# Nine second-layer products of each slot behind the join of its forms, and a new order of gathers and weight loads on GpSimd

## The chip, the cores and the metric

The kernel runs on one core of a Trainium2 chip. The metric is the device time in microseconds of one execution; the kernel before took 573.17 us (median of 3 runs, 572.85 to 578.56).

## The reference

Two stages, in fp32. First a block-local attention: q, k and v of 8 batches, 8 heads, 576 rows and head size 64; each chunk of 64 rows attends to itself alone, so a score block is 64x64. The result is laid out as x, 4608 rows of 512. Then a mixture of 8 experts, of which each row takes the one with the largest logit:

```python
logits = x @ w_gate
expert_idx = np.argmax(logits, axis=1)
gate_w = probs[np.arange(N), expert_idx]
for e in range(E):
    mask = expert_idx == e
    h = np.maximum(x[mask] @ w1[e], 0.0)      # 512 -> 1024
    out[mask] = gate_w[mask, None] * (h @ w2[e])   # 1024 -> 512
```

How many rows each expert gets is known only while the kernel runs.

## The kernel before, in words

The first 150 us do the attention, the routing and a scatter of the rows of x into a DRAM table sorted by expert (`xd`). What follows is a loop over **slots**, unrolled in the program: slot u takes 256 rows of one expert through both layers, and the last slot of an expert takes up to 192 leftover rows with them. Every operand is split into a high and a low fp32r part, so that a product of matrices is three products: hi x hi, hi x lo, lo x hi.

The code of a slot has four **forms**, of which a branch at its start picks one by the number of leftover rows (`kind`): `form_x` for 128 leftover rows (called EXT below), for 192 (EXW), for 64 (HALF), and `form_a` without any. They stand in the program in this order, and after them comes the **common part**, where the four join. In a form, first-layer columns f = 0 to 7 are computed one after another (`gemm1`, L674, or `gemm1_x`, L681; 12 matmuls each), ScalarE makes `hh` (relu, L701) and VectorE `hl` (L706) of each, and the second-layer products of column f - 2 (`block`: for each of two row halves m, three matmuls of 512 columns, L767 to L769, into psU or psV) stand between. Columns 4 and 5 (`block(4)`, `block(5)`, six matmuls each) end the form. The common part holds columns 6 and 7 of the first half (six matmuls); those of the second half (`rest`) stand in the next slot, behind its branch, for slots below 12 (`SMIN`), and in the common part from 12 on. An EXT or EXW form ends with a jump (L1317) over the forms behind it to the common part, HALF with one at L1316, `form_a` falls through. The branch at a slot's start is L1315.

In the run that is profiled, `form_a` is taken by slots 2, 3, 4, 6, 8, 11, 13, 14 and 15, HALF by 1, 5 and 7, EXW by 9 and 12, EXT by 10.

Each engine runs its own instructions in the order of the program (a manual schedule). The rows of slot u + 2 are gathered on GpSimd (`gather(u + 2)`, two indirect DMAs into `xg4[:, 2:4]`, L600), and the leftover rows of slot u + 1 too (`gather_x(u + 1)`, into `xg3` and `xg5`, L600). `load_w(u, c)` (L573) is one indirect DMA for 1 MB of weights into `raw[c]`; ScalarE and VectorE split them (L82, L83) in `split_step` and in the common part. `spread(u + 1)` at a slot's start is 16 DMAs of the SP queue (L643) that rearrange `xg4[:, 2:4]` into `xg4[:, 0:2]`; `turn` (L649, VectorE, at f = 5) transposes the latter, and `make_xs` (L654, L655) in the common part splits it into `xhl`, the input of the next slot. So `gather(u + 2)` can only start once `spread(u + 1)` has been read out. For slot 2, the common part of slot 1 uses transposes on TensorE (`make_xt(2)`, L625) in place of `turn` and `make_xs`. The leftover rows go through TensorE transposes at the start of a form (L663).

GpSimd also issues the outputs (`finish`, L799) and has a `drain` at the start of the common part. DMA completions of GpSimd are counted on eight semaphores in turn; a reader waits for the count of the one that its DMA got.

Of the kernel before, what the change touches and what calls it, by code (L numbers as in the profile page):

```python
# [40 lines left out]
XW = D + 16  # L41
HB = 3
WARM = 36
PLACE = {1: 87, 2: 110, 3: 110}
BLOCK = 256
SKEW = 128
BIG = 1.0e6
# [3 lines left out]
def attn_moe_kernel(ctx: ExitStack, tc: tile.TileContext, q, k, v, wg, w, w0, out):  # L51
# [27 lines left out]
    def split_chunk(par, c):  # L79
        hi, lo = w_hi[par][c], w_lo[par][c]  # L80
        src = raw[c // 2][:, (c % 2) * 1024:(c % 2 + 1) * 1024]
        nc.scalar.copy(hi, src)  # L82
        nc.vector.tensor_tensor(lo, src, hi.bitcast(F32), ALU.subtract)  # L83
# [20 lines left out]
    def bank(tag, shape):  # L104
        n = 1
        for x in shape[1:]:
            n *= x
        if tag == "S":
            t = psum[0].tile([P, 512], F32, name="psS", tag="S", bufs=2)
        else:  # L110
            t = slots[tag][turns[tag] % len(slots[tag])]
            turns[tag] += 1
        t = t[0:shape[0], 0:n]
        if len(shape) == 3:
            t = t.rearrange("p (a b) -> p a b", b=shape[2])
        return t
# [451 lines left out]
    def wset(u):  # L568

        return 0 if u < 2 else (u + 1) % 2  # L570

    def load_w(u, c):
        nc.gpsimd.indirect_dma_start(  # L573
            out=raw[c][:, :], out_offset=None,
            in_=w, in_offset=bass.IndirectOffsetOnAxis(ap=widx[:, u, c:c + 1], axis=0),
            bounds_check=4 * E * P - 1, oob_is_err=False)
# [10 lines left out]
    def rows_of(u):  # L587
        return xg[0] if u in (0, 2) else xg[1]
# [9 lines left out]
    def rows_in(t, u, h):  # L598
        rows = TE[u] * P if u < 2 and h < 2 else NT
        nc.gpsimd.indirect_dma_start(  # L600
            out=t[:, :], out_offset=None, in_=xd[0:rows, :],
            in_offset=bass.IndirectOffsetOnAxis(ap=place(u, h)[0:t.shape[0], :], axis=0),
            bounds_check=rows - 1, oob_is_err=False)

    def gather(u):
        for h in range(2):
            rows_in(rows_of(u)[h], u, h)

    def gather_x(u):
        rows_in(xg3, u, 2)  # L610
        rows_in(xg5, u, 3)
# [25 lines left out]
    def spread(u):  # L637

        for h in range(2):
            ids(u, rows_of(u)[h], h)  # L640
        for a in range(4):
            for b in range(4):
                nc.sync.dma_start(  # L643
                    xq.rearrange("p (h a) x -> p h a x", a=4)[b * 32:(b + 1) * 32, :, a, :],
                    xg4[a * 32:(a + 1) * 32, 2:4, b * P:(b + 1) * P])
# [77 lines left out]
    def slot_0():  # L723

        py = None
        for i, step in enumerate(BLOCKS):
            f = BLOCKS[:i].count(step)
            flush()
            if step == "1":
                ph = bank("S", [P, BLK])  # L730
                gemm1_pe(0, f, ph, range(2))
                yield
                gemm1_pe(0, f, ph, range(2, 4))
                lo_.append((ph, relu_hi(ph)))
            else:
                if py is None:
                    py = [bank(x, [P, D]) for x in "UV"]
                gemm2(0, f, h0[f], 0, py)
                if f == 7:
                    finish(0, 0, py[0])  # L740
                    last.append(py)
                    return
                yield
                gemm2(0, f, h0[f], 1, py)
            yield
# [13 lines left out]
    fill, halves = slot_0(), [2 * len(BLOCKS)]  # L759

    def gemm2(par, f, h, m, py):
        gemm2_pe(par, f, *(x[:, m * P:(m + 1) * P] for x in h), py[m])
# [41 lines left out]
    def split_step(u, i):  # L804

        if i < 2:
            if u < 2:
                load_w(u + 1, 2 + i)
                return
            split_chunk(wset(u), 6 + i)  # L810
            if i == 1:
                load_w(u + 1, 3)
                load_w(u + 1, 2)
        else:
            split_chunk(wset(u + 1), i - 2)
            if i % 2:
                load_w(u + 2, i // 2 - 1)
# [40 lines left out]
    def find_u(u):  # L858
        return find(idx[u % 3], rowm[:, u, :], rowm[:, u, :], KB - 1) if u < NU else iter(())
# [353 lines left out]
    h_of = h0[5:8] + h0[5:8] + [[hq.tile([P, BLK], F32R, name=f"{x}{f}") for x in ("hh", "hl")] for f in (6, 7)]  # L1213
# [7 lines left out]
    def slot(u, kd, nxt, left=None):  # L1221
        par = wset(u)
        py = [bank("UV"[m], [P, D]) for m in range(2)]
        if u > 1:
            spread(u + 1)

        def block(f, h, ms=(0, 1)):
            for m in ms:
                gemm2(par, f, h, m, py)

        def later():

            if u == 1:
                yield from slot_kinds()
                yield "v"
                yield from places()
            yield from find_u(u + 3)

        def some(x, n):
            for _ in range(n):  # L1240
                next(x, None)

        def form_a():
            if u == 1:
                rest_0()
            if left is not None:
                rest(u - 1, left)
            h = []
            x = later()
            for f in range(8):  # L1250
                h.append(gemm1(par, f, *h_of[f]))
                if f == 4 and u + 1 < SMAX:

                    hint(u + 1, kind_of(u + 1, PE) if u == 1 else nxt)
                if f == 0 and u > 1:
                    gather_x(u + 1)
                if f == 5 and u > 1:
                    turn()
                    gather(u + 2)
                if f < 7:  # L1260
                    if f < 6:
                        split_step(u, f)
                    some(x, 5 if u == 1 else 1)
                if 1 < f < 6:
                    block(f - 2, h[f - 2])
            assert next(x, 0) == 0
            for f in (4, 5):
                block(f, h[f])

        def form_x(n):  # L1270

            make_xt_x(u, n)
            if u == 1:
                rest_0()
            if left is not None:
                rest(u - 1, left)
            pe = [bank(x, [P, D]) for x in ("K", "Q")[0:-(-n // EXT)]]

            h = []
            x = later()  # L1280

            def more(f):
                gemm2_x(par, f, h[f][1], pe)

            for f in range(8):
                h.append(gemm1_x(par, f, n, *h_of[f]))
                if f == 4 and u + 1 < SMAX:
                    hint(u + 1, kind_of(u + 1, PE) if u == 1 else nxt)
                if f == 0 and u > 1:
                    gather_x(u + 1)  # L1290
                if f == 5 and u > 1:
                    turn()
                    gather(u + 2)
                if f < 7:
                    if f < 6:
                        split_step(u, f)
                    some(x, 5 if u == 1 else 1)
                if 1 < f < 5:
                    block(f - 2, h[f - 2][0])
                if 1 < f < 7:  # L1300
                    more(f - 2)
                if f == 4 and n > EXT:
                    nc.tensor.addr_align(BLOCK, offset=PLACE[u if u == 1 else 3 if u >= SMIN - 1 else 2], max_nops=0)
            assert next(x, 0) == 0
            more(5)
            block(3, h[3][0])
            more(6)
            more(7)
            for f in (4, 5):
                block(f, h[f][0])  # L1310
            for i, p in enumerate(pe):
                m = min(EXT, n - i * EXT)
                finish(u, 2 + i, p, m)

        with tc.If(kd > 0, label=f"kind{u}") as c:  # L1315
            with tc.If(kd > 1, label=f"half{u}") as c2:  # L1316
                with tc.If(kd < 3) as c3:  # L1317
                    form_x(EXT)
                with c3.Else():
                    form_x(EXW)  # L1320
            with c2.Else():
                form_x(HALF)
        with c.Else():
            form_a()

        nc.gpsimd.drain()
        if u == 1:
            make_xt(u + 1)
        else:
            make_xs()  # L1330
        for c in (4, 5):
            split_chunk(wset(u + 1), c)
        for f in (6, 7):
            block(f, h_of[f], (0,))
        finish(u, 0, py[0], on_act=True)
        if u + 1 < SMIN:
            return py
        rest(u, py)
# [54 lines left out]
```

## Time and profile before

| what | value |
|---|---|
| time, median of 3 runs | 573.17 us |
| the profiled execution: its time, its span | 576.16 us, 574.3 us |
| granted clock, mean over the span | 0.991 |
| TensorE busy | 556.0 us (97%) |
| VectorE, ScalarE, GpSimd busy | 426.1, 281.8, 270.3 us |
| slots | from about 150 us to 568 us |

The profiled execution stands 3.0 us above the median of the timed runs. A matmul's end is modelled in the profile, so gaps between matmuls are read from start to start. "issue" as a releaser says that nothing that the profile shows was waited for. Rows with a q behind the engine's name are its sequencer's.

### The profile page before, as it was taken

How to read it: one execution, taken by the hardware profiler on the slowest of the kernel's cores; microseconds unless marked ns; L12 is line 12 of the kernel's file. 1: busy time of each engine (PE TensorE's matmuls, PEld its weight loads, DVE VectorE, ACT ScalarE, POOL GpSimd, SP SyncE). 2: the span in 40 equal slices, each digit the busy share in tenths (PEclk: the TensorE clock that was granted, in tenths of full speed). 3: DMA queues.
4: the chain of work that ended last, by engine and by line, in shares of the span. 5: the costliest groups of instructions: out<-in, count | busy, mean ns of one | idle time of the engine just before them, and what ended most of it. 6: DMA issues, size and time to landing. Idle time of an engine off the chain costs nothing.

```text
span 574.3 us, 13260 instructions
## 1 busy us (share of the span) xinstructions
PE 556.0 (97%) x4858; PEld 489.8 (85%) x4858; DVE 426.1 (74%) x840; ACT 281.8 (49%) x548; POOL 270.3 (47%) x293
## 2 busy tenths in 40 slices
PE   7999999979999999999999999999998999999995
PEld 6788888878898888999898898888988888899894
DVE  8899999976695878776787588645665765588775
ACT  1667766743244464554654454424443542356553
POOL 6025743387643655525473574523514252274352
PEclk9999999989999999999999999999998999999998
DMA  8999999435584453456145636644622652232021
GB/s 267 406 394 352 370 356 365 156 143 199 158 323 141 142 189 91 139 190 215 47 144 166 205 93 207 227 139 136 210 63 82 203 178 94 60 104 80 19 62 38
DMA packets 49038, 102.70 MB, mean 179 GB/s; under 512 B 14176, under 2 KB 28512, under 8 KB 45312
## 3 DMA queue, kind: packets, MB, share of 16 engines
q0 software_dynamic: 19776, 61.14, 31.2%
q1 hardware_dynamic: 29120, 39.88, 20.6%
q8 instruction: 63, 1.03, 0.8%
q14 instruction: 79, 0.65, 0.4%
HBM read 113.75 MB, written 19.56 MB: 232 GB/s over the span
## 4 chain that ended last, share of the span: by engine, by line
PE 57%; issue 10%; DMA 6%; POOL 3%; DVE 2%; POOLq 0%; ACT 0%; DVEq 0%
PE psS L674 11%; PE psS L681 11%; DMA xg<-xd,idx 5%; PE psV L767 4%; PE psV L769 4%; PE psV L768 4%; PE psU L769 4%; PE psU L768 4%; PE psU L767 4%; PE psL L681 3%; PE psL L674 3%; POOL xg L600 1%; POOL raw L573 1%; PE psK L785 1%; PE psK L787 1%
## 5 line engine op out<-in xcount | busy, mean ns | idle before, releaser
L83 DVE TENSOR_TENSOR wlo<-raw,whi 128x1024 fp32r<-128x1024 f32 x118 | 142.3, 1216 | 17.7 <-ACT whi L82 17.4
L82 ACT CAST whi<-raw 128x1024 fp32r<-128x1024 f32 x118 | 121.9, 1046 | 2.8 <-DMA raw<-in_w,widx 2.8
L701 ACT ACTIVATE hh<-psS 128x256 fp32r<-128x256 f32 x98 | 37.7, 384 | 158.0 <-PE psS L674 83.1
L573 POOL DMA_INDIRECT raw<-in_w,widx x62 | 70.0, 1129 | 93.9 <-DVE wlo L83 63.7
L799 POOL DMA_INDIRECT out_y<-y,oid x40 | 51.7, 1293 | 110.0 <-issue 28.3
L674 PE MATMUL psS<-xhl,whi 128*128 128x256 f32 x496 | 93.6, 288 | 3.2 <-DVE xhl L628 2.9
L600 POOL DMA_INDIRECT xg<-xd,idx x68 | 79.8, 1173 | 27.3 <-issue 17.3
L674 PEld LDWEIGHTS psS<-xhl,whi 128*128 128x128 f32 x496 | 81.4, 195 | 7.6 <-issue 4.2
L706 DVE SCALAR_TENSOR_TENSOR hl<-psS,hh 128x256 fp32r<-128x256 f32 x98 | 41.1, 421 | 59.2 <-ACT xx L685 37.8
L674 PE MATMUL psS<-xhl,wlo 128*128 128x256 f32 x248 | 71.1, 286 | 0.0
L681 PE MATMUL psS<-xhl,whi 128*128 128x320 f32 (+2 forms) x288 | 59.8, 333 | 0.5 <-ACT xhl L665 0.5
L681 PEld LDWEIGHTS psS<-xhl,whi 128*128 128x128 f32 x288 | 49.6, 188 | 4.6 <-ACT xhl L665 0.6
L767 PE MATMUL psV<-whi,hh 128*128 128x512 f32 x128 | 51.1, 399 | 2.3 <-issue 2.3
L769 PE MATMUL psU<-whi,hl 128*128 128x512 f32 x128 | 50.2, 392 | 0.3 <-DVE hl L706 0.3
L767 PE MATMUL psU<-whi,hh 128*128 128x512 f32 x128 | 50.4, 394 | 0.0
L768 PE MATMUL psU<-wlo,hh 128*128 128x512 f32 x128 | 50.4, 393 | 0.0
L768 PE MATMUL psV<-wlo,hh 128*128 128x512 f32 x128 | 50.1, 391 | 0.0
L769 PE MATMUL psV<-whi,hl 128*128 128x512 f32 x128 | 50.1, 391 | 0.0
L674 PEld LDWEIGHTS psS<-xhl,wlo 128*128 128x128 f32 x248 | 48.4, 195 | 0.0
L447 POOL DMA_INDIRECT xd<-xb,di x32 | 31.6, 988 | 17.4 <-issue 10.6
L90 POOL TENSOR_TENSOR wlo<-raw,whi 128x512 fp32r<-128x512 f32 x16 | 20.2, 1276 | 40.9 <-DMA spare<-in_k 23.8
L767 PEld LDWEIGHTS psV<-whi,hh 128*128 128x128 f32 x128 | 24.1, 188 | 8.6 <-issue 3.1
(257 smaller groups left out, 1151.7 us busy)
## 6 DMA issues: line engine op xcount, KB each, us to landing
qt<-in_q SPq DMA_DIRECT2D x17, 512.0 KB
xg<-xg SPq DMA_DIRECT2D x224, 32.0 KB
vb<-in_v SPq DMA_DIRECT2D x12, 512.0 KB
kb<-in_k SPq DMA_DIRECT2D x22, 256.0 KB
raw<-in_w SPq DMA_DIRECT2D x16, 256.0 KB
spare<-in_k SPq DMA_DIRECT2D x12, 256.0 KB
spare<-in_v SPq DMA_DIRECT2D x6, 512.0 KB
xg<-xd,idx POOLq DMA_INDIRECT x68, 3.6
```

Source lines behind the costliest of these rows:

```text
L82: nc.scalar.copy(hi, src)
L83: nc.vector.tensor_tensor(lo, src, hi.bitcast(F32), ALU.subtract)
L573: nc.gpsimd.indirect_dma_start(out=raw[c][:, :], out_offset=None, in_=w, in_offset=bass.IndirectOffsetOnAxis(ap=widx[:, u, c:c + 1], axis= ...
L600: nc.gpsimd.indirect_dma_start(out=t[:, :], out_offset=None, in_=xd[0:rows, :], in_offset=bass.IndirectOffsetOnAxis(ap=place(u, h)[0:t.sha ...
L674: nc.tensor.matmul(ph, a, b[:, kc, 0:BLK], start=kc + i == 0, stop=kc + i == 5)
L681: nc.tensor.matmul(ph, a[par][kc][:, f * 128:(f + 1) * 128], b[:, kc, 0:BLK + n], start=kc + i == 0, stop=kc + i == 5)
L701: nc.scalar.activation(hh, ph, AF.Relu)
L706: nc.vector.scalar_tensor_tensor(hl, ph, 0.0, hh.bitcast(F32), ALU.max, ALU.subtract)
L767: nc.tensor.matmul(py, hh, wh, start=f == 0, stop=False)
L768: nc.tensor.matmul(py, hh, wl, start=False, stop=False)
L769: nc.tensor.matmul(py, hl, wh, start=False, stop=f == 7)
L799: nc.gpsimd.indirect_dma_start(out=outs[m], out_offset=bass.IndirectOffsetOnAxis(ap=oid[u % 3][0:n, m:m + 1], axis=0), in_=y, in_offset=No ...
```

## The change

Three things move; no arithmetic is added or removed.

1. In all four forms, `block(4)` keeps its first half (three matmuls into psU), and its second half and the whole of `block(5)`, nine matmuls, go to the common part, behind `make_xs` (in slot 1 behind `make_xt(2)`) and ahead of columns 6 and 7.
2. `gather_x(u + 1)` leaves f = 0 and `gather(u + 2)` leaves f = 5. Both are issued at f = 1, behind the slot's second split: `load_w(u + 1, 3)`, first half of `gather(u + 2)`, `load_w(u + 1, 2)`, `gather_x(u + 1)`, second half of `gather(u + 2)`. Slots 0 and 1 are not touched by this.
3. `PLACE`, the offset at which a piece of TensorE's code is placed within 256 instructions, is raised by 36 for each kind of slot.

```diff
-PLACE = {1: 87, 2: 110, 3: 110}
+PLACE = {1: 123, 2: 146, 3: 146}
...
-    def gather(u):
-        for h in range(2):
+    def gather(u, halves=(0, 1)):
+        for h in halves:
             rows_in(rows_of(u)[h], u, h)
...
             if i == 1:
                 load_w(u + 1, 3)
+                gather(u + 2, (0,))
                 load_w(u + 1, 2)
+                gather_x(u + 1)
+                gather(u + 2, (1,))
...
-                if f == 0 and u > 1:
-                    gather_x(u + 1)
                 if f == 5 and u > 1:
                     turn()
-                    gather(u + 2)
...
-            for f in (4, 5):
-                block(f, h[f])
+            block(4, h[4], (0,))
...
-            for f in (4, 5):
-                block(f, h[f][0])
+            block(4, h[4][0], (0,))
...
         for c in (4, 5):
             split_chunk(wset(u + 1), c)
+        block(4, h_of[4], (1,))
+        block(5, h_of[5])
         for f in (6, 7):
             block(f, h_of[f], (0,))
```

TensorE's instructions at the end of form EXT of slot 10, up to the jump to the common part (whi_6 and wlo_6 hold the second-layer weights of columns 4 and 5; a row with hl is the third product of a group). Before:

```order
L767 MATMUL psK<-whi_7_2778,xx 128x512
L768 MATMUL psK<-wlo_7_2786,xx 128x512
L769 MATMUL psK<-whi_7_2778,xx 128x512
L767 MATMUL psU<-whi_6_2777,hh 128x512
L768 MATMUL psU<-wlo_6_2785,hh 128x512
L769 MATMUL psU<-whi_6_2777,hl 128x512
L767 MATMUL psV<-whi_6_2777,hh 128x512
L768 MATMUL psV<-wlo_6_2785,hh 128x512
L769 MATMUL psV<-whi_6_2777,hl 128x512
```

and, behind these, six more for column 5 and L1317. With the change:

```order
L767 MATMUL psK<-whi_7_2778,xx 128x512
L768 MATMUL psK<-wlo_7_2786,xx 128x512
L769 MATMUL psK<-whi_7_2778,xx 128x512
L767 MATMUL psU<-whi_6_2777,hh 128x512
L768 MATMUL psU<-wlo_6_2785,hh 128x512
L769 MATMUL psU<-whi_6_2777,hl 128x512
L1312 UNCONDITIONAL_BRANCH
```

The jump (now line 1312) comes nine matmuls sooner in TensorE's stream. The common part of the same slot on TensorE, up to the branch of slot 11, before:

```order
L767 MATMUL psU<-whi_7_2778,hh_2853 128x512
L768 MATMUL psU<-wlo_7_2786,hh_2853 128x512
L769 MATMUL psU<-whi_7_2778,hl_2854 128x512
L767 MATMUL psU<-whi_7_2778,hh_2855 128x512
L768 MATMUL psU<-wlo_7_2786,hh_2855 128x512
L769 MATMUL psU<-whi_7_2778,hl_2856 128x512
L1206 TENSOR_LOAD kind
L1315 COMPARE_AND_BRANCH
```

and with the change, the piece that now stands ahead of these six:

```order
L767 MATMUL psV<-whi_6_2777,hh 128x512
L768 MATMUL psV<-wlo_6_2785,hh 128x512
L769 MATMUL psV<-whi_6_2777,hl 128x512
L767 MATMUL psU<-whi_6_2777,hh 128x512
L768 MATMUL psU<-wlo_6_2785,hh 128x512
L769 MATMUL psU<-whi_6_2777,hl 128x512
L767 MATMUL psV<-whi_6_2777,hh 128x512
L768 MATMUL psV<-wlo_6_2785,hh 128x512
L769 MATMUL psV<-whi_6_2777,hl 128x512
```

Between the two branches stand fifteen matmuls in place of six; the order of the matmuls among themselves is what it was. GpSimd in `form_a` of slot 4 (xg3 and xg5 take the leftover rows of slot 5, xg4 the rows of slot 6, raw3 and raw2 weights of slot 5, raw0 and raw1 of slot 6). Before:

```order
L600 DMA xg3_65<-xd_63,idx_2_282 128x528
L1389 ISA
L600 DMA xg5_66<-xd_63,idx_2_282 64x528
L573 DMA raw3_2770<-in_w,widx_279 128x2048
L573 DMA raw2_2769<-in_w,widx_279 128x2048
L573 DMA raw0_67<-in_w,widx_279 128x2048
L582 COMPARE_AND_BRANCH
L582 UNCONDITIONAL_BRANCH x2
L600 DMA xg4_64<-xd_63,idx_0_280 128x528 x2
L573 DMA raw1_68<-in_w,widx_279 128x2048
```

With the change:

```order
L573 DMA raw3_2770<-in_w,widx_279 128x2048
L1386 ISA
L600 DMA xg4_64<-xd_63,idx_0_280 128x528
L573 DMA raw2_2769<-in_w,widx_279 128x2048
L600 DMA xg3_65<-xd_63,idx_2_282 128x528
L600 DMA xg5_66<-xd_63,idx_2_282 64x528
L600 DMA xg4_64<-xd_63,idx_0_280 128x528
L573 DMA raw0_67<-in_w,widx_279 128x2048
```

The first half of the gather into xg4 now has raw2, xg3 and xg5 behind it in GpSimd's queue.

## Rows read from the trace of the kernel before

**Rows 1.** The page, parts 1 and 2: busy us (share), and granted clock by 40 slices.

```profile
PE 556.0 (97%) x4858; PEld 489.8 (85%) x4858; DVE 426.1 (74%) x840; ACT 281.8 (49%) x548; POOL 270.3 (47%) x293
...
PEclk9999999989999999999999999999998999999998
```

**Rows 2.** Waits of TensorE: total us, times, longest us.

```profile
PE psT L663 <- DMA out_y<-y,oid: 0.6, 1, 0.6
...
PE psU L769 <- DVE hl L706: 0.3, 1, 0.3
```

**Rows 3.** Timeline of TensorE between slots 10 and 11: start us, us, instruction.

```profile
428.89 0.39 PE L767 MATMUL psU<-whi,hh 128*128 128x512 f32 x1
...
430.02 0.39 PE L769 MATMUL psU<-whi,hl 128*128 128x512 f32 x1
432.72 0.50 PE L767 MATMUL psV<-whi,hh 128*128 128x512 f32 x1 [2.31 <-issue]
```

**Rows 4.** Line 1317, TensorE's sequencer, 424 to 429 us: ns min/median/max, start.

```profile
L1317 PEldq COMPARE_BRANCH  x1: 3768/3768/3768, 424.8 to 424.8; - x1
```

**Rows 5.** Line 1315, TensorE's sequencer, 428 to 433 us.

```profile
L1315 PEldq COMPARE_BRANCH  x1: 3513/3513/3513, 429.1 to 429.1; - x1
```

**Rows 6.** Line 1315, TensorE's sequencer, 497 to 501 us.

```profile
L1315 PEldq COMPARE_BRANCH  x1: 2404/2404/2404, 497.7 to 497.7; - x1
```

**Rows 7.** Chain of waits: start us, us, what.

```profile
434.49 4.25 PE psS L674 x24
...
450.03 2.87 PE psS L674 x24
```

**Rows 8.** Windows: us, busy us (count) by engine, granted clock, DMA share, GB/s.

```profile
434.20:437.50 3.30, 3.30 (x17) 3.22 (x16) 0.75 (x1) 0.36 (x2) 2.42 (x3) 0.50 0.46 152
```

**Rows 9.** Timeline of TensorE between slots 9 and 10.

```profile
395.36 0.39 PE L769 MATMUL psU<-whi,hl 128*128 128x512 f32 x1
396.35 0.72 PE L663 MATMUL psT<-ident,xg 128*128 128x128 f32 x4 [0.60 <-DMA out_y<-y,oid]
```

**Rows 10.** Timeline of TensorE between slots 12 and 13.

```profile
499.63 0.39 PE L769 MATMUL psV<-whi,hl 128*128 128x512 f32 x1
500.26 0.47 PE L674 MATMUL psS<-xhl,whi 128*128 128x256 f32 x2 [0.24 <-PE psV L769]
```

**Rows 11.** Timeline at the end of slot 1 (HALF), all engines.

```profile
177.71 0.39 PE L769 MATMUL psU<-whi,hl 128*128 128x512 f32 x1
...
178.07 0.68 DVE L793 TENSOR_TENSOR y<-psK,y 64x512 f32<-64x512 f32 x1 [2.29 <-ACT y L792]
...
178.79 0.48 DVE L794 TENSOR_SCALAR y<-y,gate 64x512 f32<-64x512 f32 x1
```

**Rows 12.** Timeline of VectorE at the end of form_a, slot 15.

```profile
563.23 0.42 DVE L706 SCALAR_TENSOR_TENSOR hl<-psS,hh 128x256 fp32r<-128x256 f32 x1 [0.27 <-ACT hh L701]
```

**Rows 13.** Timeline of TensorE there: third product of block(5).

```profile
564.46 0.39 PE L769 MATMUL psU<-whi,hl 128*128 128x512 f32 x1
```

**Rows 14.** Timeline of SP, slot 3: the 16 DMAs of a spread.

```profile
208.27 10.89 SPq L643 DMA_DIRECT2D xg<-xg  x16
```

**Rows 15.** Timeline of SP, slot 4.

```profile
226.33 10.58 SPq L643 DMA_DIRECT2D xg<-xg  x16
```

**Rows 16.** Timeline of GpSimd, slot 3: the two gathers behind that spread.

```profile
221.36 1.00 POOL L600 DMA_INDIRECT xg<-xd,idx  x1 [0.98 <-issue]
222.66 1.00 POOL L600 DMA_INDIRECT xg<-xd,idx  x1 [0.30 <-issue]
```

**Rows 17.** Tile xg on GpSimd, 206 to 229 us: from issue to landing.

```profile
DMA to landing us min/median/max: 3.3/3.3/3.3
```

**Rows 18.** Timeline of VectorE, slot 4: the turn.

```profile
243.09 2.07 DVE L649 STREAM_TRANSPOSE y<-xg 128x1024 f32<-128x1024 f32 x1
```

**Rows 19.** Timeline of TensorE at the start of slot 5 (HALF).

```profile
250.46 0.69 PE L663 MATMUL psT<-ident,xg 64*128 64x64 f32 x4
```

**Rows 20.** Timeline of ScalarE, common part of slot 4: raw2's two splits.

```profile
247.77 2.00 ACT L82 CAST whi<-raw 128x1024 fp32r<-128x1024 f32 x2
```

More of the change, by code (lines that the diff above doesn't have):

```diff
@@ L1288, in form_x @@
                     hint(u + 1, kind_of(u + 1, PE) if u == 1 else nxt)
-                if f == 0 and u > 1:
-                    gather_x(u + 1)
                 if f == 5 and u > 1:
                     turn()
-                    gather(u + 2)
                 if f < 7:
```

## The prediction

> **What bounds the kernel now.** The page's first two parts come first: TensorE is busy 556.0 us of the span of 574.3, and its granted clock is full but for a few slices [rows 1]. VectorE, the next, has 426.1. So only what lets TensorE stand still or run slowly in the slots can be won or lost. Since the ends of matmuls are modelled, I went through TensorE's matmuls from start to start, asked the list of waits what ended each gap, and opened the timeline there.
>
> The largest gap lies between slots 10 and 11. The last matmul of slot 10's common part starts at 430.02, the first of slot 11 at 432.72, where 0.23 would do: 2.47 us of standing still, ended by "issue" [rows 3]. TensorE's sequencer explains it. EXT's jump to the common part, L1317, starts at 424.8 and takes 3.77 us [rows 4]; the branch into slot 11, L1315, starts at 429.1 and takes 3.51 us, so to 432.66 [rows 5]. While a jump is under way no matmul enters the queue, and TensorE lives on those it already has. The six of the common part start at 428.89 to 430.02, one each (430.02 - 428.89) / 5 = 0.226 us [rows 3]. They came in after the first jump and cover little of the second. Then the granted clock is 0.50 (1.2 GHz) from 434.20 to 437.50 [rows 8], and 24 first-layer matmuls take 4.25 us there where the same group takes 2.87 at 450.03 [rows 7].
>
> Three smaller gaps follow. 395.36 to 396.35, in which slot 10's transposes of leftover rows wait 0.60 for "DMA out_y" [rows 2, 9]; their data is there, but the gather's completion is counted on the semaphore that a later output used too. 499.63 to 500.26, where the branch L1315 of 2.40 us from 497.7 ends [rows 6, 10]. And slot 1's end, where a product waits 0.3 for VectorE's `hl` [rows 2].
>
> **The change part by part.** *The nine products.* They cost the same in either place; what changes is what TensorE holds in its queue during the two jumps. L1317 comes nine matmuls sooner, L1315 stays where it is among the matmuls, so 9 x 0.226 = 2.03 us more work stands between the two. At 430 the gap shrinks from 2.47 to 0.44 us. Bounds: nothing saved, if the second jump just starts later by as much as the work between, and 2.47. I take 2.03, because the first jump then starts and ends 2.0 us earlier, while TensorE still has the queue that it had: no gap is seen ahead of the common part now, though L1317 takes 3.77 us [rows 4], and the second jump follows its fifteen matmuls by a few issues.
>
> The clock: 4.25 - 2.87 = 1.38 us [rows 7] hang on the gap of 2.47. The gaps of 395 and 500, 0.76 and 0.40 over the normal step [rows 9, 10], were followed by no slow stretch; 0.44 is nearest to them, so I take 1.38 saved (bounds 0 and 1.38).
>
> At 500, nine more matmuls stand between L1317 and L1315, 2.03 us against a gap of 0.40 [rows 10]: all 0.40 goes (bounds 0 and 0.40).
>
> A rule speaks against this part. The Trainium skill, page "Runtime: NRT & Kernel Launch", section "Instruction fetch mechanics", says that a taken branch to a target outside the two pages held makes the engine fetch that page before it goes on. By it both jumps stay far jumps, the change removes neither, and if TensorE paid for both fetches nothing would be saved at 430 and 500. The trace agrees that both jumps are long, 3.77 and 3.51 us [rows 4, 5], but TensorE stood still for only 2.47 of these 7.28 us [rows 3], so what counts is the work in its queue.
>
> *PLACE.* Eighteen instructions (nine weight loads, nine matmuls) leave the form and eighteen come in behind it; the offset of 36 puts what stands behind on the same places of the instruction blocks. I cost it at nothing; were it wrong, some other branch would lengthen, and the 0.40 of 500 is the smallest size seen for that.
>
> *The join.* In the common part `block(5)` waits for the whole of what VectorE did in the form, not for its own `hl` alone. In `form_a` VectorE's last `hl` ends at 563.23 + 0.42 = 563.65 [rows 12], and the third product of `block(5)` starts at 564.46 [rows 13]: 0.81 us to spare, no cost. In HALF the last operation of VectorE is L794, to 178.79 + 0.48 = 179.27; the product would start six steps after 177.71, at 179.07 [rows 11]. That is 0.2 us late in slot 1; slots 5 and 7 have the same code, and I take 0.1 each for them and count slot 1 below, so 0.2 in all (0 to 0.5). Behind the waiting product stand all later ones of TensorE, so it is lost in full.
>
> *Slot 1.* Its transposes (L625) now go ahead of the nine, and can meet VectorE's L793 and L794 [rows 11] up to 0.8 us too early; in return `xhl` of slot 2 is ready 2 us sooner and the wait of 0.3 for `hl` [rows 2] has work ahead of it. Net loss 0.1 (-0.3 to 0.5).
>
> *Gathers and loads.* No DMA is added. The first half of the gather into `xg4` now stands ahead of raw2, `gather_x` and raw0, and it waits for all 16 DMAs of `spread`; behind it wait all of these. Slot 3 gives the delay: its spread is issued from 208.27 for 10.89 us, to 219.16 [rows 14], and the first half starts at 221.36 [rows 16]: 2.20 after. In slot 4 the spread ends at 226.33 + 10.58 = 236.91 [rows 15], so the first half goes out at 239.11, and at 1.30 per DMA [rows 16] raw2 at 240.4, the two `gather_x` at 241.7 and 243.0. With the 1.0 of the issue and 3.3 to landing [rows 17] the leftover rows are there at 246.0; TensorE asks at 250.46 [rows 19]: 4.4 us to spare. raw2 is split at 247.77 [rows 20], 6 us after its issue ends. `turn` at 243.09 [rows 18] comes 6.2 us after the spread. So no cost. A gain: the outputs no longer follow the leftover gather on the same of the eight semaphores; the weight loads and the first half do, which are long done when TensorE asks. The 0.76 of 395 goes (floor 0). SP's spreads start with the gathers that feed them, no later than now.
>
> Sum: 2.03 + 1.38 + 0.40 + 0.76 = 4.57 saved, 0.2 + 0.1 lost, net 4.3. The profiled execution, 576.16, would become 571.9; it stands 3.0 above the median of 573.17, which becomes **568.9 us**.
>
> **Rivals.** *More than that*: the gap at 430 goes whole (0.44 more), slot 1 gains 0.3 where I took a loss, and the join costs nothing: about 567.9, and less if small gaps that I did not price close too. For it: the earlier first jump may end before TensorE's queue is short. Against: fifteen matmuls are 3.4 us, the second jump 3.5.
>
> *No cover*: the second jump starts later by what is put ahead of it, as the fetch rule would have it. Then 0.76 alone is saved and 0.3 lost: 572.7. Against it, the queue read above.
>
> *The join bites in every form*: were VectorE in `form_a` later by the two `y` operations that HALF has there, 0.68 + 0.48 = 1.16 [rows 11], TensorE would wait 1.16 - 0.81 = 0.35 in nine slots, 3.2 us: 572.1. Against it, nothing in the change lengthens VectorE's queue.
>
> *Slower*: `gather_x` behind the spread comes too late for the transposes of the next slot's leftover rows. It decides when a spread ends more than 4.4 us later against its slot than slot 4's does, which a late gather of the slot before would bring about, and it feeds itself, since that late start delays the next gather. A late landing of the size of the gap at 430 costs 2.47, and the clock 1.38, 3.85 at each of the five seams with leftover rows from slot 5 on (5, 7, 9, 10, 12): 19, so 588. For it: five transfers hang on one wait now; slot 3's spread was issued at 208.27, slot 4's at 226.33, not at one distance from their slots. Against: the gathers themselves go out sooner.
>
> **How the numbers follow.** Forecast (567.6 to 570.4, by the bounds of the costs) 0.60; more than that 0.15; no cover 0.12; the join 0.06; slower 0.07. The range takes all but the slower case and half of the best: 567.0 to 573.2. A measurement of this kernel can tell about 1% from no change, 567.4 to 578.9: faster 0.16 (the best case, and the edge of the forecast), same 0.77, slower 0.07.
>
> **What the changed profile would show.** Fifteen matmuls between the two branches at 430 and a gap of about 0.4 us in place of 2.47, with the branches as long as now; a granted clock of 1.00 behind it, and 24 first-layer matmuls in 2.87. No gap at 500, no wait of L663 for an output at 395. GpSimd's first half about 2.2 us behind the last DMA of a spread, and `gather_x` landed before L663 in slots 5 and 7. I would be wrong if the second branch's start moved with the matmuls, if waits for VectorE of over 0.3 us showed at the third product of `block(5)` in `form_a`, or if L663 waited for its gather.

## The result: 0.6% slower, outside the range

| | before | with the change |
|---|---|---|
| time, median | 572.2 us (22 runs) | 576.4 us (22 runs) |
| ratio to before, 95% interval | | 1.0059, 1.0036 to 1.0081 |
| profiled execution: time, span | 576.16, 574.3 us | 577.09, 575.3 us |
| first transpose of leftover rows (L663, slot 1) to the last matmul, start to start | 415.3 us | 413.3 us |
| last matmul's start to the end of the span | 6.4 us | 11.1 us |

Forecast were 568.9 us, range 567.0 to 573.2. The ratio leaves out executions more than 1.5% above the fastest of their kernel (with the change 581.49 and 608.19 us), so it is not the quotient of the two medians. In these two profiles the slots became 2.0 us shorter and the end of the kernel 4.7 us longer; with the second profiles of both kernels, below, 0.4 us are left of the first and all of the second. Line numbers of after: the jumps L1317 and L1315 are L1312 and L1310, the drain L1326 is L1321.

**What was meant to go.** The list of TensorE's waits after the change (columns as in [rows 2]):

```profile
PE psS L681 <- DVE gate L616: 1.4, 2, 0.8
...
PE psV L767 <- issue: 0.9, 1, 0.9
...
PE psQ L663 <- DMA xg<-xd,idx: 0.6, 1, 0.6
```

The waits for `out_y` and for `hl` [rows 2] are gone, the one by "issue" has shrunk; those of L681 for VectorE's gate and of L663 for a gather are new. TensorE's timeline at the end of slot 10, which answers to [rows 3]:

```profile
426.65 0.39 PE L769 MATMUL psU<-whi,hl 128*128 128x512 f32 x1
427.90 0.50 PE L767 MATMUL psV<-whi,hh 128*128 128x512 f32 x1 [0.87 <-issue]
...
431.21 0.39 PE L769 MATMUL psU<-whi,hl 128*128 128x512 f32 x1
431.44 0.39 PE L767 MATMUL psV<-whi,hh 128*128 128x512 f32 x1
```

and its two jumps, by line (ns, start):

```profile
L1312 PEldq COMPARE_BRANCH  x1: 3628/3628/3628, 424.2 to 424.2; - x1
```

```profile
L1310 PEldq COMPARE_BRANCH  x1: 2637/2637/2637, 428.4 to 428.4; - x1
```

The second jump costs nothing now: the fifteen matmuls from 427.90 to 431.21 outlast it, and slot 11 follows at 431.44. It is also shorter, 2.64 us where it took 3.51 [rows 5]; at its old length it would have ended at about 428.4 + 3.5 = 431.9 and left a gap of some 0.5 us (an estimate from these rows). What is left, 427.90 - 426.65 - 0.23 = 1.02 us, stands ahead of the common part, behind the first jump. The granted clock is 1.00 there.

No gap is left at slot 13's start, where [rows 10] had one. There the branch has all but gone: 0.48 us in place of 2.40 [rows 6].

```profile
L1310 PEldq COMPARE_BRANCH  x1: 478/478/478, 494.4 to 494.4; - x1
```

In all ten profiles with products moved, here and below, these two branches take 2.55 to 2.97 and 0.48 to 1.54 us; in the three with the products at their old place 3.10 to 3.51 and 2.40 to 2.88. The offset `PLACE` moved together with the products in each of them, so which of the two shortens the branches is open.

**What came instead, between slots.** GpSimd in slot 4 (timeline; half 0, raw2, two leftover gathers, half 1; the halves are the two DMAs of `gather(u + 2)`):

```profile
241.60 1.02 POOL L600 DMA_INDIRECT xg<-xd,idx  x1 [6.65 <-issue]
242.92 1.00 POOL L573 DMA_INDIRECT raw<-in_w,widx  x1 [0.30 <-issue]
244.22 1.25 POOL L600 DMA_INDIRECT xg<-xd,idx  x1 [0.30 <-PE psS L674]
245.78 1.45 POOL L600 DMA_INDIRECT xg<-xd,idx  x1 [0.31 <-issue]
247.53 1.77 POOL L600 DMA_INDIRECT xg<-xd,idx  x1 [0.30 <-issue]
```

GpSimd stands for 6.65 us until the spread has been read out, and half 1 goes out at 247.53. Before, it went out at 242.01:

```profile
242.01 1.00 POOL L600 DMA_INDIRECT xg<-xd,idx  x1 [0.31 <-issue]
```
 With the change VectorE reads that half at the start of slot 5, in the same queue ahead of the split L666 that slot 5's leftover rows need:

```profile
251.69 0.15 DVE L616 COPY gate<-xg 128x1 f32<-128x1 f32 x1 [2.00 <-DMA xg<-xd,idx]
251.76 0.15 DVE L617 SCALAR_TENSOR_TENSOR oid<-msk,xg 128x1 int32<-128x1 f32 x1
252.39 0.42 DVE L666 TENSOR_TENSOR xhl<-psT,xhl 128x256 fp32r<-128x256 f32 x1 [0.48 <-issue]
```

and TensorE waits for that:

```profile
252.87 1.44 PE L681 MATMUL psS<-xhl,whi 128*128 128x320 f32 x8 [0.62 <-DVE gate L616]
```

Slot 7 has the same. In slot 9 the late one is the second leftover gather (xg5): it went out at 351.91, landed 4.1 us later, and TensorE's transposes wait for it.

```profile
356.04 0.69 PE L663 MATMUL psQ<-ident,xg 64*128 64x64 f32 x4 [0.57 <-DMA xg<-xd,idx]
```

From start to start the three new stalls of slots 5, 7 and 9 are 0.78, 0.92 and 0.75 us over the usual step.

**And at the end.** GpSimd in slot 15 with the change, the timeline to the last output:

```profile
556.02 1.01 POOL L600 DMA_INDIRECT xg<-xd,idx  x1 [4.00 <-issue]
...
561.92 1.76 POOL L600 DMA_INDIRECT xg<-xd,idx  x1 [0.30 <-issue]
563.99 0.99 POOL L573 DMA_INDIRECT raw<-in_w,widx  x1 [0.30 <-DVE wlo L83]
565.29 1.00 POOL L573 DMA_INDIRECT raw<-in_w,widx  x1 [0.30 <-issue]
569.22 1.03 POOL L799 DMA_INDIRECT out_y<-y,oid  x1 [2.94 <-issue]
570.56 1.00 POOL L799 DMA_INDIRECT out_y<-y,oid  x1 [0.31 <-issue]
```

before the change:

```profile
559.57 1.01 POOL L600 DMA_INDIRECT xg<-xd,idx  x1 [0.31 <-issue]
562.90 0.99 POOL L573 DMA_INDIRECT raw<-in_w,widx  x1 [2.32 <-DVE wlo L83]
567.89 1.02 POOL L799 DMA_INDIRECT out_y<-y,oid  x1 [4.00 <-ACT y L796]
569.32 1.00 POOL L799 DMA_INDIRECT out_y<-y,oid  x1 [0.40 <-DVE y L798]
```

The drain between them, after and before:

```profile
L1321 POOLq DRAIN  x1: 8960/8960/8960, 559.4 to 559.4; - x1
```

```profile
L1326 POOLq DRAIN  x1: 2775/2775/2775, 562.7 to 562.7; - x1
```

Before, GpSimd was idle when TensorE ended (last matmul at 567.86), and the output went out for ScalarE's `y`. Now the last matmul starts at 564.22, and the output leaves 5.00 us later: the drain runs to 568.33, past the landing of the last of seven transfers at 567.88, and no slot of this run will read any of them.

### The profile page after: what moved, and what is told of

The parts are those of the page before. It is cut to its first block, busy times and chain, and to the rows that moved or that the text cites. A ratio compares the mean times of both kernels' runs of the same rounds, so it can differ in the third digit from the quotient of the medians.

```text
span 575.3 us, 13269 instructions
## 1 busy us (share of the span) xinstructions
PE 553.6 (96%) x4858; PEld 487.7 (85%) x4858; DVE 424.8 (74%) x840; ACT 282.1 (49%) x548; POOL 273.3 (47%) x293
## 4 chain that ended last, share of the span: by engine, by line
PE 62%; DMA 11%; SPq 9%; issue 8%; DVE 4%; POOL 2%; ACT 2%; POOLq 2%; DVEq 0%; ACTq 0%
PE psS L681 10%; SPq L643 9%; PE psS L674 7%; DMA xg<-xd,idx 6%; PE psS L251 6%; DMA xg<-xg 5%; PE psL L681 3%; PE psU L306 3%; PE psV L767 3%; PE psV L768 3%; PE psV L769 3%; PE psU L768 2%; PE psU L767 2%; PE psU L769 2%; PE psL L674 2%
## 5 line engine op out<-in xcount | busy, mean ns | idle before, releaser
L573 POOL DMA_INDIRECT raw<-in_w,widx x62 | 74.6, 1203 | 52.9 <-DVE wlo L83 24.0
L799 POOL DMA_INDIRECT out_y<-y,oid x40 | 49.4, 1235 | 104.4 <-ACT xx L685 28.3
L674 PE MATMUL psS<-xhl,whi 128*128 128x256 f32 x496 | 91.6, 284 | 0.4 <-ACT at L298 0.4
L674 PEld LDWEIGHTS psS<-xhl,whi 128*128 128x128 f32 x496 | 79.9, 191 | 4.5 <-ACT at L298 0.7
L681 PE MATMUL psS<-xhl,whi 128*128 128x320 f32 (+2 forms) x288 | 60.1, 333 | 1.8 <-DVE gate L616 1.4
L681 PEld LDWEIGHTS psS<-xhl,whi 128*128 128x128 f32 x288 | 49.4, 188 | 6.7 <-DVE gate L616 1.9
L681 PE MATMUL psS<-xhl,wlo 128*128 128x320 f32 (+2 forms) x144 | 30.4, 332 | 0.0
```

Of the source, the lines that this page charges most:

```text
L573: nc.gpsimd.indirect_dma_start(out=raw[c][:, :], out_offset=None, in_=w, in_offset=bass.IndirectOffsetOnAxis(ap=widx[:, u, c:c + 1], axis= ...
L674: nc.tensor.matmul(ph, a, b[:, kc, 0:BLK], start=kc + i == 0, stop=kc + i == 5)
L681: nc.tensor.matmul(ph, a[par][kc][:, f * 128:(f + 1) * 128], b[:, kc, 0:BLK + n], start=kc + i == 0, stop=kc + i == 5)
L799: nc.gpsimd.indirect_dma_start(out=outs[m], out_offset=bass.IndirectOffsetOnAxis(ap=oid[u % 3][0:n, m:m + 1], axis=0), in_=y, in_offset=No ...
```

## The experiments

The times vary by some 2 us from run to run, and the first 150 us, which nothing here alters, by up to 4.7; so each kernel is read by its ratio and by two pieces of its profile: first L663 to last matmul, and last matmul to the end.

| kernel | ratio, 95% interval | slots, us | end, us |
|---|---|---|---|
| before, again | 0.9990 (0.9961 to 1.0018) | 412.7 | 6.6 |
| the change, again | 1.0101 (1.0037 to 1.0164) | 413.8 | 11.3 |
| products alone | 0.9999 (0.9967 to 1.0030) | 411.8 | 6.7 |
| products alone, again | 0.9977 (0.9953 to 1.0001) | 411.6 | 6.4 |
| order alone | 1.0090 (1.0050 to 1.0130) | 415.8 | 11.2 |
| last slot in the old order | 1.0061 (1.0027 to 1.0095) | 417.5 | 8.6 |
| last slot without gathers and loads | 1.0034 (1.0003 to 1.0064) | 413.5 | 7.4 |
| both halves together | 1.0036 (1.0005 to 1.0067) | 415.0 | 8.2 |
| late leftover gather | 1.0048 (1.0021 to 1.0074) | 414.1 | 7.4 |
| six products, late leftover gather | 1.0050 (1.0019 to 1.0081) | 415.2 | 8.1 |
| other semaphores | 0.9962 (0.9931 to 0.9992) | 410.7 | 7.0 |

**Products alone.** Against the change:

```diff
                 load_w(u + 1, 3)
-                gather(u + 2, (0,))
                 load_w(u + 1, 2)
-                gather_x(u + 1)
-                gather(u + 2, (1,))
...
+                if f == 0 and u > 1:
+                    gather_x(u + 1)
                 if f == 5 and u > 1:
                     turn()
+                    gather(u + 2)
```

> Only the nine products move (with the offset raised by 36); gathers and loads are issued where the kernel before issues them. Theory A (the whole loss comes from the new order on GpSimd): faster than before, 568.5 to 571.5 us, the last output issued within 2 us of the last matmul's end as before, the gap at 430 down from 2.47 to about 1.0 us, the wait for the leftover rows at 395 still there. Theory B (the products behind the join cost more than they give): 574 us or more, with waits for VectorE at the first products of the common part.

Measured 0.9999: no loss, no gain that could be told. The end is as before (output 0.03 us behind the last matmul), and B is out: no wait for VectorE stands at the common part. The gap at 430 is 0.94 us and the wait of 0.61 for an output at 396.42 is there. Since the profile promised more than the timed runs gave, it ran once more with the unchanged kernel beside it.

> The kernel with the products alone once more, beside the others on one chip. By the two profiles of before, the products save between 0.8 and 3.3 us: time 0.994 to 0.9985 of before. Rival: they save nothing that can be measured, 0.9985 to 1.002, with the stall at 430 of about 1 us still there.

0.9977, interval 0.9953 to 1.0001: most likely some 1.3 us, at most 2.7; neither run excludes that nothing is gained. The second profile of before says why it is less than the sum's 2.03 + 1.38 + 0.40 = 3.8 us:

> The kernel before, unchanged, profiled a second time. Theory D (the stall of 2.47 us between slots 10 and 11 belongs to the code's place and is there in each execution, the slow clock behind it only in some): a gap of 2.3 to 2.6 us again, and from the first transposes of slot 1 to the last matmul 413.5 to 415.5 us. Theory E (the stall is an accident of the one execution, and the products had nothing to win): no gap above 1 us, and 411 to 412.5 us. Time within 0.5% of before in either case.

```profile
427.96 0.39 PE L769 MATMUL psU<-whi,hl 128*128 128x512 f32 x1
429.87 0.50 PE L767 MATMUL psV<-whi,hh 128*128 128x512 f32 x1 [1.52 <-issue]
```

In this second execution the same gap is 429.87 - 427.96 - 0.23 = 1.68 us, no slow clock follows, and slot 10's transposes do not wait for an output. Neither D nor E as put: the stall is there each time, its size is not, and the piece of the slots was 412.7. The 576.16 us on which the sum was made was a long execution, 3 us above the median, and much of these 3 us was what the sum booked as savings: 2.47 - 1.68, 1.38 of clock and 0.76 make 2.9, less 0.57 by which the gap at 500 is longer in the second execution (0.97 for 0.40). So the forecast took some 2.4 us (an estimate from these two executions) off twice, once as savings and once as the distance from the median.

**Order alone.** The old PLACE and the nine products in the forms, the new order on GpSimd.

> Only the order of gathers and loads changes; the nine products stay in the forms. Theory A: slower than before by what the order costs, 4.6 us behind the last matmul plus 2.3 us at slots 5, 7 and 9, less the 0.7 of 395: 576 to 579 us, the last two outputs issued 5 us or more after the last matmul. Theory B: 571 to 573 us.

1.0090, as A has it: the outputs leave 5.14 us behind the last matmul, and the wait of 395 is gone. So the loss belongs to the order. Of A's 2.3 us between the slots only slot 5's 0.80 shows here, none at slots 7 and 9. Whether the products take something off the loss (1.0090 to 1.0059) the intervals leave open.

**The last slot.** Two kernels ask how much of it lies at the end. In one, slot 15 alone has the old order; in the other it issues none of these transfers:

```diff
             if i == 1:
+                if u < 15:
                 load_w(u + 1, 3)
                 gather(u + 2, (0,))
...
-            if i % 2:
+            if i % 2 and u < 15:
                 load_w(u + 2, i // 2 - 1)
```

(the five issues behind the new condition stand one step further in).

> The change, but the last slot (15) issues its gathers and loads in the order of before. Theory A1 (most of the loss lies behind the last matmul, since GpSimd's drain waits for the late gathers and the outputs stand behind it): the first of the last two outputs is issued at about 564 us instead of 569.2, and the time falls by 4 to 5 us against the change, to 571 to 572.5. Theory A2 (the loss lies between the slots, in waits for late gathers at slots 5, 7 and 9, and the end only follows): 575 us or more.

> The change, but slot 15, the last one that these data have, issues no gathers and no weight loads for the slots behind it (they are not there in these data). Theory A1 (GpSimd's queue alone holds the last outputs): first of the last two outputs within 0.2 us of the last matmul's start instead of 5.0 behind it, the end 6.5 us behind it instead of 11.1, time 4 to 5 us below the change: 571 to 573. Theory A2 (the end is late for another reason): the tail stays at 10 us or more.

Without the transfers the outputs leave 0.03 us behind the last matmul, and 7.4 us in place of 11.1 remain: that the queue held them is shown. The time fell less than expected, from 1.0059 to 1.0034, 1.4 us of some 3.7; the intervals overlap, and against the 1.0101 of the change's second run it would be 3.8 us: how much of the end's loss the timed runs see stays open to that extent. With the old order in the last slot the outputs were still 2.49 us late and the time did not fall (median 578.0). GpSimd came late out of slot 14, where half 0 had waited for its spread till 543.0: slot 14's drain let its outputs out at 555.2, and behind them slot 15's transfers followed one another from 558.5 to 569.8. The expectation of 571 to 572.5 was wrong: it cured the last slot alone, and in this profile a late queue is handed on. (Its profiled execution is one of its longest, 582.4 against a median of 578.0; of its slots nothing is concluded.)

**The second profile of the change.**

> The changed kernel, unaltered, profiled a second time. Theory A: the outputs of the last slot are again issued 4 to 6 us behind the last matmul, the end again 10 to 12 us behind it, and waits of 0.6 to 1.9 us stand again at the first products of slots 5 and 7. Rival (the late outputs are an accident of one execution): tail below 8 us.

5.20 us, an end of 11.3, stalls of 0.86 and 0.94 at slots 5 and 7, and slot 9's wait for xg5 (0.82): no accident.

**Both halves together.**

```diff
                 load_w(u + 1, 3)
-                gather(u + 2, (0,))
                 load_w(u + 1, 2)
+                gather(u + 2)
                 gather_x(u + 1)
-                gather(u + 2, (1,))
```

> The change, but both halves of the gather stand together, ahead of the leftover gathers and behind both weight loads (w3, w2, half 0, half 1, leftover rows). Theory A (the second half comes too late: the next spread and VectorE's gates wait for it): the second half is issued 4 us sooner, the waits of 0.7 to 0.9 us at slots 5, 7 and 9 go, spreads begin when turn ends, and the end is no longer held up: 567.5 to 570.5 us. Theory C (any gather at f = 1 behind the spread holds up GpSimd's queue, whatever its order): 574 to 577 us.

The waits of slots 5, 7 and 9 go, and the output is late by 1.01 us only: the second half was what slots 5 and 7 waited for, and slot 9's xg5 goes out at 346.39 in place of 351.91, though it still stands behind both halves. But the time is 1.0036, since a wait of 2.5 us stands at slot 10's start, where xhl of the leftover rows is missing (and one of 1.0 us for `hl` in slot 13). The next kernel has the wait of slot 10 too.

**Late leftover gather.** The old place for `gather`, and `gather_x(u + 1)` behind the two weight loads.

> The nine products behind the join as in the change; of the new order only this is kept, that the leftover gather is issued behind the slot's second split and both weight loads; the gather into xg4 stays at the sixth column. Theory A (what hurts is the first half that waits for the spread ahead of everything): no waits of L681 at slots 5, 7 and 9, last output issued right behind the last matmul, no wait for an output at 395: from slot 1 to the last matmul 411 us, the end 6.5 us behind it, time 569 to 571.5, the same as or up to 1 us below the kernel with the products alone. Theory C (any later leftover gather hurts): waits of over 0.7 us at the transposes or first products of slots 5, 7, 9 or 10, time 573 or more.

No waits at 5, 7 and 9, but slot 10 loses 2.6 us. ScalarE's timeline at the end of slot 9, and TensorE's:

```profile
398.70 1.99 ACT L82 CAST whi<-raw 128x1024 fp32r<-128x1024 f32 x2 [3.53 <-DMA out_y<-y,oid]
```

```profile
401.94 0.97 PE L681 MATMUL psS<-xhl,whi 128*128 128x384 f32 x4 [2.43 <-ACT xhl L665]
```

The leftover rows were there. ScalarE wanted raw2, issued at 368.64 and landed at 375.5, and waited for an *output*, issued at 395.65 inside form EXW and landed at 398.68. C's signs came, a wait at slot 10 and 576.7 us, but not for its reason, and A did not have this either: in this order the output of the form's second extra piece is the eighth transfer behind raw2, so both are counted on one of the eight semaphores, and a reader behind the join waits for what the form added to it. In the run with both halves together raw2 shares in the same way, and ScalarE waits 3.58 us for an output. In the kernel before it is the leftover gather that shares (the wait for `out_y` [rows 2, 9]), in the change half 0, whose reader is SP's next spread.

**Six products.** As above with `block(4)` whole in the form and PLACE raised by 24.

> As the run with the late leftover gather, but six products (column 5) move instead of nine, and the offset is raised by 24. Theory F (TensorE holds about 2.7 us of work when it meets the first jump, so that the nine starve it there by 0.95 us): the gap ahead of the common part of slot 10 shrinks by 3 x 0.226 to about 0.3 us, and a gap of at most 0.5 opens behind it at the second jump; time as the nine's or 0.5 us less. Theory G (the first gap hangs on where the jump's target lies, not on the queue): the gap ahead of the common part stays at 0.9 us or more.

TensorE's timeline at both jumps of slot 10:

```profile
429.26 0.39 PE L769 MATMUL psV<-whi,hl 128*128 128x512 f32 x1
429.97 0.50 PE L767 MATMUL psU<-whi,hh 128*128 128x512 f32 x1 [0.33 <-ACT whi L82]
...
432.60 0.39 PE L769 MATMUL psU<-whi,hl 128*128 128x512 f32 x1
433.48 0.50 PE L767 MATMUL psV<-whi,hh 128*128 128x512 f32 x1 [0.49 <-issue]
```

The gap ahead of the common part falls to 0.48 us, and 0.65 opens behind it: so G is out, and F holds in kind, with both gaps some 0.15 us above its figures. The first row names ScalarE's split, which ends at 429.90; the jump ends at 429.92, so both end this wait. 1.13 in sum against 0.8 to 1.3 with nine; where the products stand decides which jump is short of cover, and six are no better. (A wait of 2.7 us at slot 10's start is here too, as in the kernel before this, and makes the time.)

**Other semaphores.** A version made from this: products moved, `gather` at the old place, and the order such that the two outputs of EXW are the eighth behind xg5 and raw3, which nobody reads right behind the join.

```diff
                 load_w(u + 1, 3)
-                gather(u + 2, (0,))
+                rows_in(xg3, u + 1, 2)
                 load_w(u + 1, 2)
-                gather_x(u + 1)
-                gather(u + 2, (1,))
...
+                if f == 0 and u > 1:
+                    rows_in(xg5, u + 1, 3)
                 if f == 5 and u > 1:
                     turn()
+                    gather(u + 2)
```

> The nine products behind the join, and of GpSimd's order only this is altered against the kernel before: the second leftover gather (xg5) is issued first, at the first column, and the leftover gather into xg3 between the loads of raw3 and raw2; the gather into xg4 stays at the sixth column. The two outputs inside a form EXW then share their completion semaphores with xg5 and raw3, which nobody reads right behind the join. Theory H (a reader behind the join waits for every DMA counted on its semaphore inside the form, also for outputs): no wait of 2.6 us for xhl at the start of slot 10 as with the late leftover gather, none of 0.6 to 0.8 for an output at 395 as before; from slot 1 to the last matmul 410.5 to 412, the end 6.5 us behind it, time 570 to 573. Theory C (the later leftover gather itself is late): the wait of 2.6 us stays, time 575 or more.

TensorE at the start of slot 10:

```profile
392.83 0.39 PE L769 MATMUL psU<-whi,hl 128*128 128x512 f32 x1
393.06 0.63 PE L663 MATMUL psT<-ident,xg 128*128 128x128 f32 x4
```

No wait there, nor at slot 10's first products; the gap of 0.93 us at slot 10's end, ahead of the common part, remains. The slots take 410.7 us, and the ratio is 0.9962, interval 0.9931 to 0.9992: the lowest of all, 0.1 to 0.7% below before, and 1.0 to 1.4% below the change (its two ratios are 1.0059 and 1.0101). The products alone, beside it in the same series, took 572.95 us (median) against 570.60. H holds where it was tried, in slots 9 and 10.

## Why the prediction was wrong

**The step that failed** is *Gathers and loads*, "So no cost". It followed the transfers to three readers (the transposes of the leftover rows, raw2's split, `turn`), and for when they are read by the times of one slot, 4. The change hit three readers that it did not follow, and one of the three in another slot.

*The second half.* The prediction let it go out behind the two leftover gathers and asked only when these must land. And SP's spreads were to start "no later than now". Half 1 has two readers: VectorE's gates (L616) at a slot's start, and the next spread on SP, which needs both halves. By its own numbers it would have gone out at 244.3, 2.3 us later than before. It went out at 247.53: the spread began at 227.63 and lasted 11.56 us where 226.33 and 10.58 were taken from [rows 15], half 0 followed it by 2.41 where 2.20 was taken, and the issues took 1.25 to 1.77 us in place of 1.0 [rows 16].

*The circle.* Half 1 lets the next spread begin, the spread lets the next half 0 begin, and two transfers more now stand between the halves. SP with the change in slots 14 and 15:

```profile
520.93 10.82 SPq L643 DMA_DIRECT2D xg<-xg  x16
```

```profile
542.39 11.21 SPq L643 DMA_DIRECT2D xg<-xg  x16
```

21.5 us from one to the next, and a slot of `form_a` takes 22.5 (519.45 to 541.95, first-layer matmuls). From slot 13's spread (497.86) to slot 14's it was 23.1. So a spread that is late at slot 13 has won back next to nothing by slot 15. Before, the spread of slot 15 began as soon as `turn` let it (536.68 + 2.08):

```profile
538.79 11.25 SPq L643 DMA_DIRECT2D xg<-xg  x16
```

With the change TensorE is 3 us ahead, `turn` ends at 535.63, and the spread begins 6.8 us behind it, 0.1 us behind the landing of half 1. The same shows in GpSimd's waits of all gathers, after and before (us, times, longest):

```profile
POOL xg L600 <- issue: 62.6, 48, 7.2
```

```profile
POOL xg L600 <- issue: 17.3, 54, 1.0
```

*The outputs.* Behind the waiting half 0 the prediction named raw2, `gather_x` and raw0, and not the drain and the outputs that follow in the same queue. In the slots the outputs stand behind the drain too, and no wait of TensorE in the list names them; behind the last slot they are the end of the kernel: 11.1 - 6.4 = 4.7 us, the largest piece.

*The leftover rows.* "4.4 us to spare" was slot 4's figure. There the transposes asked at 248.80, 1.7 us behind the landing of what was issued at 244.22; in slot 9 the rows came too late, by the 0.75 us above.

*The semaphores.* "the weight loads and the first half do, which are long done when TensorE asks" looked at TensorE; SP asks for the first half. Its spread in slot 13 began at 497.86, when the output issued at 493.80 had landed, instead of 491.20; TensorE lost nothing by it directly, but the late spreads of slots 14 and 15 follow on it (no run takes this wait away by itself). In SP's waits after the change the line (us, times, longest)

```profile
SPq L643 <- DMA out_y<-y,oid: 45.2, 2, 33.1
```

is new; of before there is none.

Apart from this step the base was wrong, as above: what the sum saved was partly the long execution's own.

**The others.** *Slower* was the right rival, with the wrong price and mostly the wrong reader: it looked at `gather_x` and at 3.85 us a seam; measured were 0.78 and 0.92 us at slots 5 and 7 for half 1, 0.75 at slot 9 for `gather_x` itself, no slow clock, and an end that it did not have. *Nine products at 430*: 0.44 us were forecast to remain, 1.02 do. The reason given, that TensorE "still has the queue that it had", is wrong: L1312 starts at 424.2 and the matmuls ahead of it last to 426.65 + 0.23, 2.7 us, where before they lasted from 424.8 [rows 4] to 428.89 [rows 3], 4.1 us. Nor did the first jump start 2.0 us earlier: it started at 424.2 in place of 424.8, while TensorE was equally far in both profiles (the product that starts at 426.65 with the change started at 426.62 before). Why the jump does not move with the matmuls is open. The second jump costs nothing, by the matmuls that cover it and by its being 0.87 us shorter, which was not forecast ("with the branches as long as now"). The Trainium skill's rule that the prediction cites ("Runtime: NRT & Kernel Launch", section "Instruction fetch mechanics"), that a branch out of the pages held waits for a fetch, agrees with the jumps at 430, which stay long at 3.63 and 2.64 us; that nothing could be saved on them is not what the rows show. *The clock*: 1.00 as forecast, but slow in only two of three profiles with the products at their old place. *500*: gone, but by luck: the sum had the branch covered by nine matmuls, and the branch itself fell from 2.40 to 0.48 us. *395*: gone, but it was not in each execution of before. *The join*: forecast 0.1 us each in slots 5 and 7, measured none. *Slot 1*: the second group of transposes waits 0.43 us, and the wait for `hl` is gone, so nothing in sum, as forecast.

Sum by the profiles, means of two each: slots 414.0 before and 413.6 after, end 6.5 and 11.2; together 4.3 us, and the timed runs give 0.0059 x 572.2 = 3.4 (2.1 to 4.6).

## What to carry to other kernels

When a transfer is put ahead of others in an in-order queue, follow every transfer behind it to its reader, on all engines, and the queue to the kernel's last output; if one of those readers feeds the transfer that is waited for, add the circle up and set it against the period of the loop. Where completions are counted on a few semaphores in turn, a reader behind a join of branches waits for the branch's own transfers on that semaphore too: count which transfer comes how many places behind, and let them share with something that nobody reads there. A profiled execution above the median of the runs can hold accidents, and a saving that is an accident's size may not be there in the others: look at a second one first.

## What was not expected of the hardware

The first jump of slot 10 took 3.43 to 3.95 us over the thirteen profiles, and the gap between slots 10 and 11, with the products at their old place, 1.68, 2.47 and 2.51 us. A standstill of about 2.5 us brought the slow clock in some profiles only: it followed 2.47 us at 430 [rows 8], 2.51 in the kernel with the order alone and 2.69 at slot 10's start with six products (0.50 from 398.8 to 401.0), not 2.60 in the one with the late leftover gather and 2.68 with both halves together. Windows of the kernel with the order alone and of the one with the late leftover gather (columns as in [rows 8]):

```profile
431.00:435.00 4.00, 3.77 (x13) 3.17 (x14) 0.75 (x1) 0.00 (x0) 1.00 (x1) 0.57 0.38 114
```

```profile
399.00:404.00 5.00, 2.57 (x15) 2.13 (x14) 4.01 (x10) 2.86 (x4) 1.32 (x1) 1.00 0.27 79
```

0.57 is mostly the level of 1.2 GHz, 1.00 that of 2.4 GHz. What decides whether it falls no run here shows. And the drain on GpSimd, 2.8 us at the end of before, lasted 15.57 us in slot 4 of the changed kernel,

```profile
L1321 POOLq DRAIN  x1: 15573/15573/15573, 245.0 to 245.0; - x1
```

to 260.58: it outlasted four transfers that were issued while it ran, the last of them landed at 260.13.
